# Attention units of eight heads in place of four, with the softmax denominators as products of their own

## The chip, the cores and the metric

One core of one Trainium2 chip. The metric is device time in microseconds (us) for one execution of the whole program; lower is better.

## The reference

```python
for c in range(S // 32):                      # chunked attention, B=2, H=8, S=768, D=64
    k_full = concat(mem_k, k[c*32-16 : c*32+40])   # 8 memory keys and up to 56 others
    a = exp(scale * q_c @ k_full.T - max)
    out[c] = (a / (a.sum() + 1e-9)) @ v_full
x = out as (1536 tokens, 512)
x = sum_e p[:, e] * (relu(x @ w1[e]) @ w2[e])      # 4 experts, F = 1024
h = x @ w_in                                       # 512 -> 2048
y = (max(h, 0) + alpha * min(h, 0)) @ w_out
```

All values are float32. The matrix products after attention are made from high and low parts in a reduced form of float32 (names ending in h and l), three products for each, and the first of each pair by a scheme of seven block products in place of eight, which needs sums of token blocks (`st`) and of weight blocks (`s`).

## The kernel before, in words

**Attention.** 1536 tokens are 12 units of 128 (`u`), each with 8 heads. A half unit (`half_unit`, line 221) takes four heads through these steps:

- S: 32 small matmuls on TensorE write the scores into the tile `two`, two banks of PSUM (the even heads in the first, the odd in the second), with 4 windows of 32 queries by 64 keys each. VectorE takes the maximum (`mx`) and writes the difference to `pe`.
- exp on ScalarE, in place.
- T: two transposes of `pe` into PSUM, copied to `pt` by ScalarE.
- X: 16 matmuls of `pt` with `v`. The tile of v holds a column of ones beside its 64 columns, so the denominators come out as column 64. VectorE adds 1e-9 (`dn`), inverts (`rd`) and scales to `xs`.
- XT: two transposes of `xs`, copied by ScalarE into `acc`, tokens as columns.

After the fourth half unit of a block of 256 tokens (two units, one block `c` of columns), `prep_x` (line 157) makes from `acc` the token operands `xh` and `xl` of the first expert product: ScalarE rounds, VectorE makes four sums in `st`, GpSimd (POOL) or VectorE the low parts. `pt`, `xs` and `pe` are rings of two (line 205), `qk` of four half units, `v` of three. The tile `two` is one buffer in both kernels.

**Order of the work.** Every engine executes in the order in which the program emits. `att_cycle` (line 332) emits the first part: scores of half unit m, XT of m-3, X of m-2, exp of m, then four or five filler products (`keep_warm`, line 150, whose results nobody reads), then T of m-1. It runs until the first three blocks of columns are done, which takes 16 cycles. After that the first expert tile (0, 384 columns) begins. Its 42 products of `gemm1` (line 601) and 48 of `gemm2` (line 688) each call `att_poll` (line 296) first, which emits whatever step of the remaining half units is due by a running sum of assumed costs (`now`, `T_S`, `LAT`, `PACE` and so on, lines 878 to 886). `clear` and `NEED` say which stage of one half unit has to follow which of an earlier one. The loop at line 842 drains what is left before the second tile begins.

**Queues.** All loads go out on SP's queue in program order: `load_half` (q and k of a half unit) after S, `load_v` after X, and the other tiles by the list `begun` (line 818), which counts half units begun. The first expert weights (`raw`) are prepared by POOL and ScalarE during attention (`prep_w1`, line 412).

Of the kernel before, what the change touches and what calls it, by code (L numbers as in the profile page):

```python
# [20 lines left out]
BLK = 128  # L21
# [14 lines left out]
QW, KW, VW = HP * BLK, HP * SPAN, HP * (D + 1)  # L36
# [29 lines left out]
def tile_kernel(ctx: ExitStack, tc: tile.TileContext, qk, v, wa, wq, dpt, alpha, out):  # L66
# [83 lines left out]
    def keep_warm(hu):  # L150

        o = bank(f"keep{hu}")[:, :NCOL // 2]
# [4 lines left out]
    def prep_x(c0, n, fast):  # L157
# [5 lines left out]
        e = dve if fast else pool  # L163
        sub = ALU.subtract
        act.copy(xh[:, 0:4, cs], acc[:, :, 0, cs])
        dve.tensor_tensor(out=st[:, 0], in0=b12, in1=b11, op=sub)
        yield
        dve.tensor_tensor(out=st[:, 1], in0=b22, in1=st[:, 0], op=sub)
        act.copy(xh[:, 4:6, cs], b22)
        yield  # L170
        dve.tensor_tensor(out=st[:, 2], in0=b22, in1=b12, op=sub)
        pool.tensor_tensor(out=xl[:, 0:4, cs], in0=acc[:, :, 0, cs], in1=xh[:, 0:4, cs].bitcast(F32), op=sub)
        yield
        for z in (0, 1):
            r = slice(6 + 4 * z, 10 + 4 * z)
# [8 lines left out]
            (e if fast or z else dve if c0 == 2 * BLK else pool).tensor_tensor(  # L184
                out=xl[:, r, cs], in0=t_, in1=xh[:, r, cs].bitcast(F32), op=sub)
            yield

    def transition(c0, n):
        yield now[0] + X_WAIT[c0 > 0], None
        for d0 in range(c0, c0 + n, BLK):  # L190
            for _ in prep_x(d0, BLK, True):
                yield now[0] + DT_X[c0 > 0], None

    def mm(*a, n, took=None, **kw):
# [5 lines left out]
    v_t = [bp.tile([P, 2, HP, NW, D + 1], F32, name=f"v{i}", **tag) for i, tag in enumerate(  # L200
        [dict(tag="w2", bufs=4)] * 2 + [dict(tag="fr")])]
# [3 lines left out]
    pt_ring, xs_ring, pe_ring = (bp.tile([P, 2, HP * BLK], F32, tag="ft", bufs=3, name=x) for x in ("pt", "xs", "pe"))  # L205
    pt_ring = pt_ring.rearrange("p r (z q) -> p r z q", q=BLK)
    xs_ring = xs_ring.rearrange("p r (z e d) -> p r z e d", e=2, d=D)
    pe_ring = pe_ring.rearrange("p r (z k e) -> p r z k e", e=2, k=KEYS)
# [5 lines left out]

    def load_v(hu):
        if hu >= 2 * NU:
            return
        for e in range(2):
            sync.dma_start(v_t[hu % RINGV][e::2, e].rearrange("p z w d -> p (z w d)"), v[hu // 2, e, :, hu % 2])

    def half_unit(u, half):

        hu = 2 * u + half
        qv = qk_t[hu % RING][:, :QW].rearrange("p (z q) -> p z q", q=BLK)
        kv = qk_t[hu % RING][:, QW:].rearrange("p (z k) -> p z k", k=SPAN)
        vv = v_t[hu % RINGV]
# [8 lines left out]
        for z in range(HP):
            for w in range(NW):
                for e in range(2):
                    rows = slice(e * D, (e + 1) * D)
                    mm(s_ps[win[w], e, z], qv[rows, z, win[w]], kv[rows, z, w * STEP:w * STEP + KEYS], n=KEYS,
                       took=T_S, start=True, stop=True)  # L240
        load_half(hu + RING)
        mx = cp.tile([P, 2, HP], F32, tag="mx", bufs=4, name=f"mx{nm}")
        dve.tensor_reduce(out=mx, in_=s_ps, axis=AX.X, op=ALU.max)
        pe = pe_ring[:, hu % 2]
        dve.tensor_tensor(
            out=pe.rearrange("p z k e -> p e z k"), in0=s_ps,
            in1=mx.unsqueeze(3).to_broadcast([P, 2, HP, KEYS]), op=ALU.subtract,
# [4 lines left out]
        t_ps = bank(f"t{nm}")[:, :HP * BLK].rearrange("p (z q) -> p z q", q=BLK)  # L252
        now[0] += T_SW
        for z in range(HP):
            pe_.transpose(t_ps[:, z], pe[:, z].rearrange("p k e -> p (k e)"), ident)
            now[0] += T_T
        pt = pt_ring[:, hu % 2]
        act.copy(pt, t_ps)
        yield LAT[1]
        x_ps = bank(f"x{nm}")[:, :2 * VW].rearrange("p (z e d) -> p z e d", e=2, d=D + 1)  # L260
        now[0] += T_SW
        for z in range(HP):
            for w in range(NW):
                mm(x_ps[win[w], z], pt[:, z, win[w]], vv[:, :, z, w], n=2 * (D + 1), took=T_X, start=True, stop=True)
        load_v(hu + RINGV)
        dn = cp.tile([P, HP, 2, 1], F32, tag="dn", bufs=2, name=f"dn{nm}")
        dve.tensor_scalar_add(dn, x_ps[:, :, :, D:D + 1], 1e-9)
        rd = cp.tile([P, HP, 2, 1], F32, tag="rd", bufs=2, name=f"rd{nm}")
        dve.reciprocal(rd, dn)
        xs = xs_ring[:, hu % 2]  # L270
        dve.tensor_tensor(out=xs, in0=x_ps[:, :, :, :D], in1=rd.to_broadcast([P, HP, 2, D]), op=ALU.mult)
        yield LAT[2]
        xt_ps = bank(f"xt{nm}")[:, :2 * BLK].rearrange("p (c q) -> p c q", q=BLK)
        now[0] += T_SW
        for z in range(HP):
            pe_.transpose(xt_ps[:, z], xs[:, z].rearrange("p e d -> p (e d)"), ident)
            now[0] += T_T
        act.copy(acc[:, hs, ab, cols], xt_ps)
        if ab == 1 and half == 1:
            while att["x"] < c:  # L280
                yield 0.2
            for _ in prep_x(c * BLK, BLK, c in FAST):
# [3 lines left out]
    att = {"next": 0, "start": 0.0, "done": 0, "over": set(), "live": [], "x": 0, "stage": [0] * (2 * NU + 1)}

    NEED = {0: 3, 2: 4}

    def clear(hu):  # L290
        if att["stage"][hu] == 3 and hu > 1 and att["stage"][hu - 2] < 5:
            return False
        return hu < 2 or att["stage"][hu - 2] >= NEED.get(att["stage"][hu], 0)


    def att_poll(force=False):

        while True:
            due = [x for x in att["live"] if x[0] <= now[0] and clear(x[2])]
            room = att["next"] < 2 * NU and len(att["live"]) < LIVE and clear(att["next"])  # L300
# [11 lines left out]
            elif room and att["start"] <= now[0]:  # L312
                g = half_unit(*divmod(att["next"], 2))
# [17 lines left out]

    def att_cycle():
# [14 lines left out]
        def at(hu, stage):  # L347
            if hu in live and att["stage"][hu] == stage:
                advance(live[hu])

        x = live[m] = [now[0], half_unit(*divmod(m, 2)), m]
# [100 lines left out]
    def prep_w2(p):  # L452
# [5 lines left out]
        if p == 1:  # L458
            yield pause(0.0, lambda: att["done"] == 2 * NU and (1, 1) in raws)
# [344 lines left out]
    for k in range(kc + 9, len(tiles)):  # L804
# [3 lines left out]
    load_half(0)  # L808
    load_half(1)
    load_v(0)  # L810
    load_half(2)
    load_half(3)
    load_v(1)
    load_v(2)
# [21 lines left out]
    for i, (what, k, *other) in enumerate(order):  # L836
# [3 lines left out]
        if what == 1:  # L840
            if p == 0:
                while att["done"] < 4 * -(-(c0 + n) // BLK):
# [4 lines left out]
                    prep_poll()  # L847
                    begin()
# [49 lines left out]
RINGV = 3  # L898
# [75 lines left out]
```

## Time and profile before

| | |
|---|---|
| median of 3 runs | 833.89 us (832.63 to 834.43) |
| the profiled execution's own time | 834.19 us |
| its span, first to last instruction | 832.4 us |
| granted clock of TensorE | 1.00 of full speed (2.4 GHz) |
| TensorE, VectorE, ScalarE, GpSimd busy | 98%, 71%, 40%, 68% |

The span is shorter than the time by what lies around the program. In the timelines of the profile a row gives the start, the time from there to the end of the last of its instructions, the engine, the operation with the tile that is written and those that are read, the count, and in brackets the engine's idle time before it and what ended it. TensorE's matmuls are pipelined and their ends are modelled, so the distance from one start to the next tells more than a duration. Nearly all instructions bear line 60, that of a helper which records every operation; the tiles' names tell them apart.

### The profile page before, as it was taken

To read this page: it belongs to the slowest core of one execution; us is meant where nothing else is said; L and a number is where in the kernel's file an instruction comes from. 1 tells how busy PE (TensorE), PEld (TensorE's weight loads), DVE (VectorE), ACT (ScalarE), POOL (GpSimd) and SP (SyncE) were. 2 spreads that over 40 slices of the span, in tenths; PEclk is the share of its full clock that TensorE was granted. 3 is DMA by queue.
4 is the path that set the end of the run, shared out by engine and by line. 5 is a ranking of instruction groups with operands and counts; after the bars stand their busy time and mean duration, and the time that the engine had idled before them with its cause. 6 is when DMAs were issued, how large, how long until landed. Compare 5 with 4: busy or idle time off the path is not lost.

```text
span 832.4 us, 15024 instructions
## 1 busy us (share of the span) xinstructions
PE 817.8 (98%) x5659; PEld 794.4 (95%) x5659; DVE 592.2 (71%) x1151; ACT 335.5 (40%) x754; POOL 563.0 (68%) x584
## 2 busy tenths in 40 slices
PE   9988999999999999999999999999999999999998
PEld 6656999999999999999999999999899999999998
DVE  5878656876786776876777767568964877756555
ACT  3655542322322332332232333144663756456432
POOL 2746767868878878878687773183955887866611
PEclk9999999999999999999999999999999999999999
DMA  8794102323223223223323302001002142211004
GB/s 243 214 275 121 52 26 92 102 99 101 89 65 101 89 80 124 89 64 102 102 90 102 113 27 73 30 23 54 27 4 98 52 118 74 76 53 51 1 0 152
DMA packets 30504, 71.70 MB, mean 86 GB/s; under 512 B 4704, under 2 KB 9952, under 8 KB 30432
## 3 DMA queue, kind: packets, MB, share of 16 engines
q1 hardware_dynamic: 30432, 70.75, 26.5%
q8 instruction: 44, 0.72, 0.4%
q14 instruction: 28, 0.23, 0.1%
HBM read 59.18 MB, written 11.56 MB: 85 GB/s over the span
## 4 chain that ended last, share of the span: by engine, by line
PE 86%; DVE 5%; POOL 4%; ACT 2%; issue 1%; DMA 1%; SPq 0%; DVEq 0%; POOLq 0%; ACTq 0%
PE y L60 46%; PE a L60 11%; PE c L60 11%; PE d L60 10%; PE b L60 5%; POOL xl L60 1%; DVE st L60 1%; POOL gg L60 1%; DMA raw<-in_wa 1%; POOL wl L60 1%; ACT g L60 1%; PE x L60 1%; POOL s L60 1%; PE keep L60 1%; DVE xs L60 1%
## 5 line engine op out<-in xcount | busy, mean ns | idle before, releaser
L60 PE MATMUL y<-gg,wh 128*128 128x384 f32 x1540 | 400.7, 337 | 0.6 <-POOL gg L60 0.4
L60 POOL TENSOR_TENSOR gg<-g,gg 128x384 fp32r<-128x384 f32 x192 | 202.0, 1062 | 125.0 <-ACT gg L60 112.7
L60 PEld LDWEIGHTS y<-gg,wh 128*128 128x128 f32 x1540 | 279.2, 188 | 1.8 <-POOL gg L60 1.6
L60 PE MATMUL y<-gg,wl 128*128 128x384 f32 (+1 forms) x770 | 259.2, 337 | 0.0
L60 DVE TENSOR_TENSOR acc<-y,acc 128x384 f32<-128x384 f32 x321 | 170.2, 549 | 51.0 <-PE y L60 49.4
L60 ACT CAST gg<-g 128x384 fp32r<-128x384 f32 x192 | 97.6, 511 | 171.6 <-DVE g L60 171.4
L60 POOL TENSOR_TENSOR wl<-raw,wh 128x256 fp32r<-128x256 f32 (+1 forms) x112 | 114.9, 1034 | 52.5 <-ACT wh L60 39.9
L60 PEld LDWEIGHTS y<-gg,wl 128*128 128x128 f32 x770 | 144.5, 188 | 0.0
L60 ACT COPY u<-a 128x384 f32<-128x384 f32 x48 | 23.0, 478 | 181.8 <-PE a L60 181.8
L60 POOL TENSOR_TENSOR wl<-s,wh 128x256 fp32r<-128x256 f32 x88 | 68.0, 779 | 6.9 <-ACT wh L60 6.7
L60 DVE TENSOR_TENSOR u<-b,u 128x384 f32<-128x384 f32 x48 | 26.7, 556 | 57.1 <-PE b L60 53.3
L60 PE MATMUL a<-xh,wh 128*128 128x384 f32 x184 | 62.3, 339 | 0.5 <-ACT u L60 0.5
L60 PE MATMUL d<-xh,wh 128*128 128x384 f32 x184 | 62.2, 338 | 0.0
L60 PE MATMUL a<-xl,wh 128*128 128x384 f32 x184 | 62.0, 337 | 0.0
L60 PE MATMUL a<-xh,wl 128*128 128x384 f32 x184 | 61.9, 336 | 0.0
L60 PE MATMUL d<-xh,wl 128*128 128x384 f32 x184 | 61.8, 336 | 0.0
L60 PE MATMUL d<-xl,wh 128*128 128x384 f32 x184 | 61.8, 336 | 0.0
L60 ACT CAST wh<-raw 128x256 fp32r<-128x256 f32 (+1 forms) x116 | 54.5, 491 | 14.8 <-PE y L60 14.2
L60 PE MATMUL c<-xh,wh 128*128 128x384 f32 x176 | 59.5, 338 | 0.3 <-DVE b L60 0.3
L60 PE MATMUL c<-xh,wl 128*128 128x384 f32 x176 | 59.4, 337 | 0.0
L60 POOL TENSOR_TENSOR fl<-fl,fm 128x512 f32<-128x512 f32 x32 | 41.4, 1293 | 26.4 <-DVE fm L60 17.5
L60 PE MATMUL c<-xl,wh 128*128 128x384 f32 x176 | 59.2, 336 | 0.0
(111 smaller groups left out, 1398.4 us busy)
## 6 DMA issues: line engine op xcount, KB each, us to landing
fr<-in_wq SPq DMA_DIRECT2D x32, 512.0 KB, 3.9
raw<-in_wa SPq DMA_DIRECT2D x28, 512.0 KB, 3.8
w2s<-fl SPq DMA_DIRECT2D x32, 256.0 KB, 2.4
raw<-w2s SPq DMA_DIRECT2D x16, 512.0 KB, 3.7
qk<-in_qk SPq DMA_DIRECT2D x24, 312.0 KB, 4.2
v<-in_v SPq DMA_DIRECT2D x48, 130.0 KB, 4.0
outT<-acc SPq DMA_DIRECT2D x15, 192.0 KB, 1.9
pb<-p_dram SPq DMA_DIRECT2D x6, 384.0 KB, 3.3
```

The source lines that it names most:

```text
L60: return self.tc.keep_in_program_order(f(*a, **kw))
```

## The change

- A unit of eight heads (`unit`) takes the place of two half units. Each stage has 64 matmuls, 4 transposes or 32 matmuls, and one operation of 512 columns on VectorE or ScalarE where there were two of 256. `pt`, `xs` and `pe` have one buffer each.
- v loses its column of ones. The denominators are made by matmuls of their own (D) from `pt` and a tile `sel` of two columns of ones over the even and the odd keys; units at the ends of a sequence use other columns in the first or last window, and 16 matmuls in place of four. They are written to columns 256 to 263 of the first bank of `two`, beside the scores.
- In a cycle: scores of m, D and X of m-1, exp of m, fillers (ten in the first cycle, four in the others), T of m, XT of m-1.
- The token sums `st` read XT's result in PSUM for the odd unit of a block; only two of its four rows of 128 are kept in `acc` as they are, and the last sums overwrite the other half of `acc`.
- v has four buffers for the first 16 half units and three after. The list `begun` counts units. Some constants of the emitter's costs change.

```diff
-    def keep_warm(hu):
+    def keep_warm(u):
...
-        for i in range(5 if hu < 3 else 4):
+        for i in range(4 if u else 10):
...
+    sel = []
+    for name, k0, k1 in (("inner", 0, KEYS), ("first", LEFT, KEYS), ("last", 0, KEYS - RIGHT)):
+        sel.append(cp.tile([P, 2], F32, name=name))
+        dve.tensor_reduce(out=sel[-1], in_=ident[:, 2 * k0:2 * k1].rearrange("p (k e) -> p e k", e=2),
+                                axis=AX.X, op=ALU.add)
+    pt, xs, pe = (bp.tile([P, 2 * HP * BLK], F32, tag="ft", bufs=3, name=x) for x in ("pt", "xs", "pe"))
...
+    def unit(u):
...
+        n_s = 2 * HP * KEYS
+        s_ps = two[:, :, :n_s].rearrange("p e (z k) -> p e z k", k=KEYS)
+        d_ps = two[:, 0, n_s:n_s + 4 * HP]
         now[0] += T_SW
+        for half in range(2):
...
+                        mm(s_ps[win[w], e, HP * half + z], qv[rows, z, win[w]], kv[rows, z, w * STEP:w * STEP + KEYS],
+                           n=KEYS, took=T_S, start=True, stop=True)
+            load_half(2 * u + half + RING)
+        mx = cp.tile([P, 2, 2 * HP], F32, tag="mx", bufs=2, name=f"mx{u}")
         dve.tensor_reduce(out=mx, in_=s_ps, axis=AX.X, op=ALU.max)
         dve.tensor_tensor(
             out=pe.rearrange("p z k e -> p e z k"), in0=s_ps,
+            in1=mx.unsqueeze(3).to_broadcast([P, 2, 2 * HP, KEYS]), op=ALU.subtract,
         )
         yield LATE
         act.activation(pe, pe, AF.Exp, scale=scale)
         yield LAT[0]
...
         act.copy(pt, t_ps)
         yield LAT[1]
         now[0] += T_SW
+        for z in range(2 * HP):
+            d = d_ps[:, 2 * z:2 * z + 2]
+            if 0 < j < NBLK - 1:
+                mm(d, pt[:, z], sel[0], n=2, took=T_D, start=True, stop=True)
+            else:
+                for w in range(NW):
+                    edge = 1 if j == w == 0 else 2 if j == NBLK - 1 and w == NW - 1 else 0
+                    mm(d[win[w]], pt[:, z, win[w]], sel[edge], n=2, took=T_D / NW, start=True, stop=True)
...
+                mm(x_ps[win[w], z], pt[:, z, win[w]], v_of(2 * u + half)[:, :, i, w], n=2 * D, took=T_X,
+                   start=True, stop=True)
+            if i == HP - 1:
+                while v_next[0] < V_FOUR and v_next[0] <= 2 * u + half + 4 or v_next[0] <= 2 * u + half + 3:
+                    load_v(v_next[0])
+        dve.tensor_scalar_add(dn, d_ps, 1e-9)
...
+        if ab == 0:
+            act.copy(first, xt_ps)
+            yield X_STEP[c]
             while att["x"] < c:
                 yield 0.2
+            act.copy(xh[:, 0:4, cols], first)
+            yield X_STEP[c]
+            pool.tensor_tensor(out=xl[:, 0:4, cols], in0=first, in1=xh[:, 0:4, cols].bitcast(F32), op=sub)
+            return
+        st = bp.tile([P, 3, 2, BLK], F32, tag="st", name=f"st{u}")
+        b12, b22 = xt_ps[:, 0:2], xt_ps[:, 2:4]
+        act.copy(st[:, 2], b22)
+        dve.tensor_tensor(out=st[:, 0], in0=b12, in1=acc[:, 0:2, 0, cols], op=sub)
+        if c not in FAST:
+            yield X_STEP[c]
+        dve.tensor_tensor(out=st[:, 1], in0=b22, in1=st[:, 0], op=sub)
+        act.copy(xh[:, 4:6, cols], st[:, 2])
+        dve.tensor_tensor(out=acc[:, 2:4, 1, cols], in0=st[:, 2], in1=b12, op=sub)
+        yield X_STEP[c]
...
+        (dve if c in FAST else pool).tensor_tensor(
+            out=xl[:, 10:14, cols], in0=acc[:, :, 1, cols], in1=xh[:, 10:14, cols].bitcast(F32), op=sub)
+        att["x"] = c + 1
+    NEED = {0: 3, 2: 4, 3: 5}
+    def clear(u):
+        return u == 0 or att["stage"][u - 1] >= NEED.get(att["stage"][u], 0)
...
+        x = live[m] = [now[0], unit(m), m]
...
         advance(x)
-        at(m - 3, 4)
-        at(m - 2, 3)
+        at(m - 1, 3)
         at(m, 1)
+        rest()
         keep_warm(m)
-        at(m - 1, 2)
+        at(m, 2)
+        at(m - 1, 4)
         now[0] = max(now[0], t0 + PACE0)
+        rest()
...
-LAT = (1.0, 0.8, 1.6)
-LATE = 1.3
-T_S, T_X, T_T, T_SW = 0.017, 0.06, 0.11, 0.1
-FAST = (5,)
+LAT = (1.1, 1.0, 1.9)
+LATE = 1.6
+T_S, T_X, T_T, T_SW, T_D = 0.018, 0.06, 0.11, 0.1, 0.1
+FAST = (2, 5)
-PACE = 1.9
-PACE0 = 2.2
-X_STEP = (1.2, 0.8, 0.4, 1.0, 1.0, 0.4)
-PREP0 = 13.5
+PACE = 3.8
+PACE0 = 3.9
+X_STEP = (0.8, 0.8, 0.0, 0.8, 0.8, 0.8)
+PREP0 = 11.0
-RINGV = 3
+V_FOUR = 16
```

## Rows read from the trace of the kernel before

**Rows 1.** The page: engines' busy time, granted clock by slice

```profile
PE 817.8 (98%) x5659; PEld 794.4 (95%) x5659; DVE 592.2 (71%) x1151; ACT 335.5 (40%) x754; POOL 563.0 (68%) x584
...
PEclk9999999999999999999999999999999999999999
```

**Rows 2.** Busy time by stretch: length, engines with instructions, clock, DMA share, GB/s

```profile
4.92:47.10 42.18, 38.95 (x860) 28.37 (x859) 32.00 (x86) 22.36 (x61) 21.07 (x26) 1.00 0.83 243
47.10:85.53 38.43, 33.12 (x547) 25.30 (x547) 30.85 (x74) 22.36 (x58) 22.41 (x20) 1.00 0.57 176
85.53:832.40 746.87, 741.80 (x4237) 738.19 (x4236) 527.78 (x988) 289.32 (x634) 516.14 (x528) 1.00 0.22 72
...
8.00:16.00 8.00, 7.85 (x173) 5.94 (x171) 5.11 (x17) 3.42 (x9) 0.00 (x0) 1.00 0.95 283
72.00:80.00 8.00, 5.29 (x41) 3.93 (x40) 7.70 (x15) 3.40 (x9) 5.29 (x6) 1.00 0.20 59
```

**Rows 3.** Timeline of TensorE (PE), one cycle of stage A and the scores before

```profile
11.25 0.45 PE L60 MATMUL two<-qk 64*32 64x64 f32 x32
...
13.41 0.38 PE L60 MATMUL t<-ident,pe 128*128 128x128 f32 x2
13.72 0.45 PE L60 MATMUL two<-qk 64*32 64x64 f32 x32
14.11 0.44 PE L60 MATMUL xt<-ident,xs 128*128 128x128 f32 x2
14.47 0.65 PE L60 MATMUL x<-v,pt 128*32 128x130 f32 x16
15.05 0.97 PE L60 MATMUL keep<-xh 128*128 128x384 f32 x4
15.86 0.38 PE L60 MATMUL t<-ident,pe 128*128 128x128 f32 x2
```

**Rows 4.** Timeline of TensorE: the longest wait of stage A

```profile
22.92 0.65 PE L60 MATMUL x<-v,pt 128*32 128x130 f32 x16 [1.01 <-DMA v<-in_v]
```

**Rows 5.** Waits, 0 to 90 us: us in total, times, longest

```profile
PE xt L60 <- DVE xs L60: 4.5, 7, 1.9
...
PE two L60 <- issue: 1.9, 2, 1.4
```

**Rows 6.** Chain that ended last: start, duration, two transposes and six products

```profile
13.57 0.22 PE t L60 x2
...
85.70 1.05 PE a L60 x6
```

**Rows 7.** Groups of instructions by form, 0 to 110 us: busy, mean ns, idle

```profile
L60 PE MATMUL keep<-xh 128*128 128x384 f32 x67 | 16.6, 372 | 0.0
...
L60 DVE TENSOR_TENSOR xs<-x,rd 128x256 f32<-128x256 f32 x24 | 10.2, 424 | 0.8
L60 ACT ACTIVATE pe<-pe 128x256 f32<-128x256 f32 x24 | 10.1, 419 | 12.9 <-DVE pe L60 11.2 <-DVE dn L60 1.7
...
L60 ACT CAST xh<-acc 128x512 fp32r<-128x512 f32 x6 | 3.8, 628 | 0.0
...
L60 DVE TENSOR_TENSOR t<-d,u 128x384 f32<-128x384 f32 x3 | 1.7, 554 | 0.4 <-PE d L60 0.3
```

**Rows 8.** Timelines of VectorE, and of TensorE behind one difference

```profile
11.84 0.42 DVE L60 TENSOR_REDUCE mx<-two 128x4 f32<-128x256 f32 x1 [0.80 <-PE two L60]
12.37 0.42 DVE L60 TENSOR_TENSOR pe<-two,mx 128x256 f32<-128x256 f32 x1
...
29.08 0.35 DVE L60 TENSOR_REDUCE mx<-two 128x4 f32<-128x256 f32 x1
29.46 0.42 DVE L60 TENSOR_TENSOR pe<-two,mx 128x256 f32<-128x256 f32 x1
...
29.94 0.46 PE L60 MATMUL two<-qk 64*32 64x64 f32 x32 [0.33 <-DVE pe L60]
...
43.21 1.45 DVE L60 TENSOR_TENSOR st<-acc,st 128x256 f32<-128x256 f32 x1
```

More of the change, by code (lines that the diff above doesn't have):

```diff
@@ L148, in tile_kernel, with prep_x @@
     nc.gpsimd.memset(xh[:, 10:14, spare].bitcast(F32), 0.0)
-    def keep_warm(hu):
-        o = bank(f"keep{hu}")[:, :NCOL // 2]
+    def keep_warm(u):
+        o = bank(f"keep{u}")[:, :NCOL // 2]
         now[0] += 0.1
-        for i in range(5 if hu < 3 else 4):
+        for i in range(4 if u else 10):
             mm(o, xh[:, 10 + i % 4, NCOL // 2:NCOL // 2 + P], xh[:, 13, spare], n=NCOL // 2, start=True, stop=True)
-    def prep_x(c0, n, fast):
+    def prep_x(c0, n):
         cs = slice(c0, c0 + n)
@@ L190, in transition @@
         for d0 in range(c0, c0 + n, BLK):
-            for _ in prep_x(d0, BLK, True):
+            for _ in prep_x(d0, BLK):
                 yield now[0] + DT_X[c0 > 0], None
@@ L199, in tile_kernel @@
     qk_t = [bp.tile([P, QW + KW], F32, tag="ggB", bufs=4, name=f"qk{i}") for i in range(RING)]
-    v_t = [bp.tile([P, 2, HP, NW, D + 1], F32, name=f"v{i}", **tag) for i, tag in enumerate(
-        [dict(tag="w2", bufs=4)] * 2 + [dict(tag="fr")])]
+    v_t = [bp.tile([P, 2, HP, NW, D], F32, name=f"v{i}", **tag) for i, tag in (
+        (3, dict(tag="w2", bufs=4)), (0, dict(tag="w2", bufs=4)), (1, dict(tag="w2", bufs=4)), (2, dict(tag="fr")))]
+    v_t = v_t[1:] + v_t[:1]
     for vt in v_t:
@@ L204, in tile_kernel, with v_of @@
             (pool, dve)[e].memset(vt[:, e], 0.0)
[L205 to L208, printed above, removed]
+    sel = []
[4 more added lines that the diff above has]
+    pt, xs, pe = (bp.tile([P, 2 * HP * BLK], F32, tag="ft", bufs=3, name=x) for x in ("pt", "xs", "pe"))
+    pt = pt.rearrange("p (z q) -> p z q", q=BLK)
+    xs = xs.rearrange("p (z e d) -> p z e d", e=2, d=D)
+    pe = pe.rearrange("p (z k e) -> p z k e", e=2, k=KEYS)
+    def v_of(hu):
+        return v_t[hu % 4 if hu < V_FOUR else (hu - V_FOUR) % 3]
     def load_half(hu):
@@ L218, in load_v @@
         for e in range(2):
[L219 to L226, printed above, removed]
+            sync.dma_start(v_of(hu)[e::2, e].rearrange("p z w d -> p (z w d)"), v[hu // 2, e, :, hu % 2])
+    def unit(u):
@@ L227, in half_unit @@
         c, ab = divmod(u, 2)
+        j = u % NBLK
         cols = slice(c * BLK, (c + 1) * BLK)
-        hs = slice(2 * half, 2 * half + 2)
-        nm = f"{u}_{half}"
         win = [slice(w * WIN, (w + 1) * WIN) for w in range(NW)]
-        s_ps = two[:, :, :HP * KEYS].rearrange("p e (z k) -> p e z k", k=KEYS)
+        n_s = 2 * HP * KEYS
+        s_ps = two[:, :, :n_s].rearrange("p e (z k) -> p e z k", k=KEYS)
+        d_ps = two[:, 0, n_s:n_s + 4 * HP]
         now[0] += T_SW
[L235 to L240, printed above, removed]
@@ L241, in half_unit @@
-        load_half(hu + RING)
-        mx = cp.tile([P, 2, HP], F32, tag="mx", bufs=4, name=f"mx{nm}")
+        for half in range(2):
+            qk_ = qk_t[(2 * u + half) % RING]
+            qv = qk_[:, :QW].rearrange("p (z q) -> p z q", q=BLK)
+            kv = qk_[:, QW:].rearrange("p (z k) -> p z k", k=SPAN)
+            for z in range(HP):
+                for w in range(NW):
+                    for e in range(2):
+                        rows = slice(e * D, (e + 1) * D)
+                        mm(s_ps[win[w], e, HP * half + z], qv[rows, z, win[w]], kv[rows, z, w * STEP:w * STEP + KEYS],
+                           n=KEYS, took=T_S, start=True, stop=True)
+            load_half(2 * u + half + RING)
@@ L251, in half_unit @@
         yield LAT[0]
-        t_ps = bank(f"t{nm}")[:, :HP * BLK].rearrange("p (z q) -> p z q", q=BLK)
+        t_ps = bank(f"t{u}").rearrange("p (z q) -> p z q", q=BLK)
         now[0] += T_SW
-        for z in range(HP):
+        for z in range(2 * HP):
             pe_.transpose(t_ps[:, z], pe[:, z].rearrange("p k e -> p (k e)"), ident)
             now[0] += T_T
-        pt = pt_ring[:, hu % 2]
         act.copy(pt, t_ps)
         yield LAT[1]
-        x_ps = bank(f"x{nm}")[:, :2 * VW].rearrange("p (z e d) -> p z e d", e=2, d=D + 1)
@@ L261, in half_unit @@
         now[0] += T_SW
-        for z in range(HP):
-            for w in range(NW):
[L264 to L270, printed above, removed]
@@ L271, in half_unit @@
-        dve.tensor_tensor(out=xs, in0=x_ps[:, :, :, :D], in1=rd.to_broadcast([P, HP, 2, D]), op=ALU.mult)
+        for z in range(2 * HP):
+            d = d_ps[:, 2 * z:2 * z + 2]
+            if 0 < j < NBLK - 1:
+                mm(d, pt[:, z], sel[0], n=2, took=T_D, start=True, stop=True)
+            else:
+                for w in range(NW):
+                    edge = 1 if j == w == 0 else 2 if j == NBLK - 1 and w == NW - 1 else 0
+                    mm(d[win[w]], pt[:, z, win[w]], sel[edge], n=2, took=T_D / NW, start=True, stop=True)
@@ new lines, in unit @@
+        x_ps = bank(f"x{u}").rearrange("p (z e d) -> p z e d", e=2, d=D)
+        for z in range(2 * HP):
+            half, i = divmod(z, HP)
+            for w in range(NW):
+                mm(x_ps[win[w], z], pt[:, z, win[w]], v_of(2 * u + half)[:, :, i, w], n=2 * D, took=T_X,
[3 more added lines that the diff above has]
+                    load_v(v_next[0])
@@ L272, in half_unit @@
+        dn = cp.tile([P, 4 * HP], F32, tag="dn", bufs=2, name=f"dn{u}")
+        dve.tensor_scalar_add(dn, d_ps, 1e-9)
+        rd = cp.tile([P, 2 * HP, 2, 1], F32, tag="rd", bufs=2, name=f"rd{u}")
+        dve.reciprocal(rd.rearrange("p z e o -> p (z e o)"), dn)
+        dve.tensor_tensor(out=xs, in0=x_ps, in1=rd.to_broadcast([P, 2 * HP, 2, D]), op=ALU.mult)
         yield LAT[2]
-        xt_ps = bank(f"xt{nm}")[:, :2 * BLK].rearrange("p (c q) -> p c q", q=BLK)
+        xt_ps = bank(f"xt{u}").rearrange("p (c q) -> p c q", q=BLK)
@@ L274, in half_unit @@
         now[0] += T_SW
-        for z in range(HP):
+        for z in range(2 * HP):
             pe_.transpose(xt_ps[:, z], xs[:, z].rearrange("p e d -> p (e d)"), ident)
             now[0] += T_T
-        act.copy(acc[:, hs, ab, cols], xt_ps)
-        if ab == 1 and half == 1:
+        sub = ALU.subtract
+        first = acc[:, :, 0, cols]
+        if ab == 0:
+            act.copy(first, xt_ps)
+            yield X_STEP[c]
             while att["x"] < c:
                 yield 0.2
-            for _ in prep_x(c * BLK, BLK, c in FAST):
-                yield X_STEP[c]
-            att["x"] = c + 1
@@ L286, in tile_kernel @@
[L286 to L293, printed above, removed]
+            act.copy(xh[:, 0:4, cols], first)
+            yield X_STEP[c]
+            pool.tensor_tensor(out=xl[:, 0:4, cols], in0=first, in1=xh[:, 0:4, cols].bitcast(F32), op=sub)
@@ new lines, in unit @@
+        yield X_STEP[c]
+        while att["x"] < c:
+            yield 0.2
+        act.copy(xh[:, 6:10, cols], st[:, 0:2].rearrange("p a b n -> p (a b) n"))
+        dve.tensor_tensor(out=acc[:, 0:2, 1, cols], in0=acc[:, 2:4, 0, cols], in1=st[:, 1], op=sub)
+        pool.tensor_tensor(out=xl[:, 4:6, cols], in0=st[:, 2], in1=xh[:, 4:6, cols].bitcast(F32), op=sub)
+        yield X_STEP[c]
+        pool.tensor_tensor(out=xl[:, 6:10, cols], in0=st[:, 0:2].rearrange("p a b n -> p (a b) n"),
+                           in1=xh[:, 6:10, cols].bitcast(F32), op=sub)
@@ new lines, in unit @@
+        act.copy(xh[:, 10:14, cols], acc[:, :, 1, cols])
+        yield X_STEP[c]
+        (dve if c in FAST else pool).tensor_tensor(
+            out=xl[:, 10:14, cols], in0=acc[:, :, 1, cols], in1=xh[:, 10:14, cols].bitcast(F32), op=sub)
+        att["x"] = c + 1
+    att = {"next": 0, "start": 0.0, "done": 0, "over": set(), "live": [], "x": 0, "stage": [0] * (NU + 1)}
+    NEED = {0: 3, 2: 4, 3: 5}
+    def clear(u):
+        return u == 0 or att["stage"][u - 1] >= NEED.get(att["stage"][u], 0)
@@ L299, in att_poll @@
             due = [x for x in att["live"] if x[0] <= now[0] and clear(x[2])]
-            room = att["next"] < 2 * NU and len(att["live"]) < LIVE and clear(att["next"])
+            room = att["next"] < NU and len(att["live"]) < LIVE and clear(att["next"])
             if due:
@@ L312, in att_poll @@
             elif room and att["start"] <= now[0]:
-                g = half_unit(*divmod(att["next"], 2))
+                g = unit(att["next"])
                 att["start"] = now[0] + (PACE0 if force else PACE)
@@ L339, in advance @@
             try:
-                x[0] = next(x[1]) + (now[0] if att["stage"][x[2]] < 6 else x[0])
+                x[0] = next(x[1]) + now[0]
             except StopIteration:
@@ L345, in advance, with at, rest @@
                     att["done"] += 1
[L347 to L351, printed above, removed]
+        def at(u, stage):
+            if u in live and att["stage"][u] == stage:
+                advance(live[u])
+        def rest():
+            for x in list(att["live"]):
+                if att["stage"][x[2]] > 4 and x[0] <= now[0]:
+                    advance(x)
+            prep_poll()
+            begin()
+        x = live[m] = [now[0], unit(m), m]
         att["live"].append(x)
@@ L458, in prep_w2 @@
         if p == 1:
-            yield pause(0.0, lambda: att["done"] == 2 * NU and (1, 1) in raws)
+            yield pause(0.0, lambda: att["done"] == NU and (1, 1) in raws)
         if p:
@@ L806, in tile_kernel @@
     order += [(2, len(tiles) - 1)]
[L808 to L814, printed above, removed]
+    for hu in range(RING):
+        load_half(hu)
+    for hu in range(4):
+        load_v(hu)
     stream("w", weights())
@@ L841, in tile_kernel @@
             if p == 0:
-                while att["done"] < 4 * -(-(c0 + n) // BLK):
+                while att["done"] < 2 * -(-(c0 + n) // BLK):
                     if k == 0:
@@ L846, in tile_kernel @@
                         att_poll(force=True)
-                    prep_poll()
-                    begin()
+                        prep_poll()
+                        begin()
             if k == k0 - 1:
@@ L940 @@
     qk = np.concatenate([halves(qs, BLK), halves(ks, SPAN)], axis=3)
[L941 removed]
+    vs = vs.reshape(NU, KEYS, 2, HP, 2, NW, D).transpose(0, 4, 1, 2, 3, 5, 6)
     def pairs(wi, wo):
```

45 lines of the change are left out of this document (19 added, 26 removed).

## The prediction, on record before the kernel ran

> **What bounds the kernel now.** I read the page first: TensorE is busy 98% of the span, and its granted clock is at full speed (2.4 GHz) in every slice [rows 1]. Next the three stretches into which the change divides the span [rows 2]. From 85.53 us on TensorE's gaps are short: 741.80 us busy in 746.87. That stretch holds none of the changed code, so I carry it over unchanged; what the change earns or costs must appear before 85.53 us. Stage A, 4.92 to 47.10, is attention with filler products; stage B, 47.10 to 85.53, is the rest of attention threaded through the 90 products of the first expert tile. No other engine is full in either stage (VectorE 32.00 us of 42.18 and 30.85 of 38.43).
>
> Then TensorE's timeline. A cycle of stage A is one half unit and has five groups, read from start to start [rows 3]: transposes of pe 0.31 us (13.41 to 13.72), scores S 0.39, transposes of xs 0.36, products X 0.58, four fillers 0.81: together 2.45. Two halves, one unit of eight heads, cost 4.90. Sixteen cycles run from 4.92 to 47.10; the stage's few waits are of 1 us and less, the longest for v [rows 4]. In B the gaps are larger: four of the seven waits for xs, 3.7 of their 4.5 us, and one of 1.4 that has no releaser [rows 5]; the dense work there is 8 S, 9 T, 10 X, 11 XT and 90 products at 1.05/6 = 0.175 each [rows 6]: 3.1 + 2.8 + 5.8 + 4.0 + 15.8 = 31.5. Of the 38.43 us, 5.1 are the gaps named, and 1.8 is left for changes between short groups.
>
> **Part 1: whole units.** S has 64 matmuls (2 x 0.39 = 0.77 rounded down), X 32 (1.16). Each further transpose costs 0.11 (two in 0.22 [rows 6]), so T is 0.31 + 0.22 = 0.53 and XT 0.58. Fillers stay four, 0.81, but per unit: 38 in stage A against 67 [rows 7].
>
> On VectorE a 256-wide operation takes 0.42 and a 384-wide one 0.55 [rows 7], 1.0 ns an element, so a 512-wide one 0.68. Exp on ScalarE goes from 0.42 to about 0.63, the figure of a 512-wide rounding there, and the copies with it [rows 7]. Per unit VectorE saves about 0.8 us on maxima, differences, reciprocals and scaling, and some on token sums, which it now reads half from PSUM. That relief I count at nothing on the path: VectorE needs 0.68 x 3 + 0.16 + 0.18 = 2.4 us a unit and at most three sums of 0.8, 4.8 in all, against the cycle of 5.88 below. It is covered by the wait of part 2; without that cover it would show as in rival 1.
>
> **Part 2: the denominators' products D.** This is where I expect the loss. D(m-1) writes columns 256 to 263 of the first bank of tile `two`. In program order it follows S(m), and the maximum and difference of unit m, which read that bank. If the tile is guarded as a bank, D(m-1) waits until VectorE has finished the difference of unit m. TensorE takes its instructions in order, so X(m-1), the fillers, T(m) and XT(m-1) queue behind D, and ScalarE (pt, the token copies), VectorE's xs and the v loads on SP's queue behind those.
>
> The length of that wait comes from one half unit [rows 8, 3]. S starts at 11.25, the maximum at 11.84: 0.59 later, and with 32 more matmuls 0.97. The difference starts 0.53 after the maximum; 512-wide 0.79, so at 1.76. It ends 0.68 later, at 2.44. The tightest handover from this difference to TensorE is 29.88 to 29.94, so D can begin at 2.50. S has issued by 0.77: TensorE stands 1.73 us in every unit.
>
> D itself isn't in the trace: four matmuls with 128x128 weights and 2 columns (16 with 128x32 weights in the edge units 0, 5, 6 and 11). Lower bound 0.05 (the pitch of S, 0.39/32, four times), upper bound 0.58 (16 at the pitch of X). I take 0.30, near the middle: the nearest row, a transpose at 0.11, loads the same weights but moves 128 columns. The ones column leaves X, whose pitch I keep (128 columns for 130).
>
> Cycle: 0.77 + 1.73 + 0.30 + 1.16 + 0.81 + 0.53 + 0.58 = 5.88, against 4.90. Exp has ended at 2.44 + 0.68 = 3.1, so T, reached at 4.8, waits for nothing; xs is ready 0.7 after X, within the fillers and T.
>
> **Sum of A.** Eight cycles again: unit 5 must be over before the first expert product, with its last token part on VectorE, after unit 7's T. The first cycle has no D: S, then ten fillers while exp is made, T at 3.15, end at 3.68. Seven at 5.88 make 41.2. One us I add for the three or four token sums of unit 5 that come together ahead of unit 7's maximum (one took 1.45 here [rows 8]). Together 45.9 against 42.18: **+3.7**.
>
> **Sum of B.** Left are 4 S, 4 T, 5 D, 5 X, 5 XT and the products: 3.1 + 2.1 + 1.5 + 5.8 + 2.9 + 15.8 = 31.2; changes between groups 1.0 (fewer groups). Working the emitter's costs through by hand, D(8) follows directly on S(9) (1.73), D(9) and D(10) have an XT between (1.15 each), the other two have no S before them: 4.0. VectorE also carries the expert tile there (7.70 us of 8 in its fullest stretch [rows 2]), and may be inside one operation when a maximum comes due: 0.4 on each of the three, 1.2. Of the old gaps I keep half of the 1.4 and a quarter of the waits for xs: 1.7. Together 39.1 against 38.43: **+0.6**.
>
> **Edits costed at nothing.** DMA: a unit brings 2 x 312 KB of qk and 4 x 128 KB of v, 1.16 MB; over 5.88 us that is 198 GB/s, and 283 were moved in one stretch [rows 2]. Raw weights are asked for somewhat earlier, behind four instead of three pairs of v loads, and the POOL queue that waits for them is idle then; expert weights for the next tile are asked for one half unit later, and TensorE's 90 products cover that. One more v buffer adds two memsets, and three short sums make `sel`; both run before the first scores arrive. POOL takes one 1.3 us subtraction more in the last block, off the path.
>
> 834.19 (the profiled run's own time; its span is 832.4) + 3.7 + 0.6 = 838.5. That run was 0.3 above the median of 833.89, so **838.2**.
>
> **Rival 1, faster: D doesn't wait.** D's columns are not the ones VectorE reads, and if the guard goes by columns nothing holds it. For this speaks that the fillers read `xh` with 0.0 idle while ScalarE writes other columns of the same tile [rows 7]; against it, that this tile is in SBUF, and that the trace has no product entering a part of a PSUM tile while another part is read. Then TensorE's cycle is 4.15, or 4.26 with T held until exp (3.15 + 0.06). A: 3.68 + 7 x 4.26 + 1.0 = 34.5, -7.7. B loses the 4.0: 35.1, -3.3. 834.19 - 11.0 - 0.3 = 822.9. Traffic (1.16 MB in 4.26 us = 272 GB/s) would then be the next limit. The deciding place is the start of D against the end of the difference. Chance 0.15.
>
> The Trainium skill, "PSUM — Partial Sum Buffer", section "PSUM bank collisions raise a hardware error", speaks against this change: two engines on one bank and quadrant have to be separated by a semaphore even at different columns. By that rule D waits and the sum is 838.2; without it 822.9. No row here shows it.
>
> **Rival 2, a wash: the wait is there but all my short groups are dear.** If D costs 0.05, VectorE's second operation follows 0.1 sooner (as at 29.46, 0.38 after 29.08 [rows 8]) and B's backlog and old gaps don't come back, then 12 x 0.25 + 12 x 0.1 + 1.7 = 5.9 us fall away: 832.3. The middle of that stretch, about 834, is where the removed fillers (29 x 0.2 = 5.8 us) just pay for D and the wait. For it: VectorE sets several gaps of the kernel before. Against: these were only 3.7 us in B. Chance 0.22, of it 0.13 within 0.2%, which is what a measurement can tell from no change (1.7 us), and 0.09 below.
>
> **Rival 3, much slower: the clock falls.** TensorE would stand 29% of each cycle. In 72 to 80 us it was busy 5.29 of 8 at full clock [rows 2], so I give 0.03; at 1.2 GHz some 4 us of work a unit would double, up to +30 us, about 868.
>
> **How the numbers follow.** Forecast (bank guarded, over 0.2% slower) 0.60, rival 1 0.15, rival 2 0.22, rival 3 0.03. Slower 0.63, same 0.13, faster 0.24. The forecast alone spans 835.6 to 844 (D at 0.58 in twelve units, +3, and another 2 to 3 of backlog). The range goes down to 826, so that it holds rival 2 and leaves rival 1 and the far end out.
>
> **What would show it.** Right: in the waits, D on TensorE ended by VectorE's difference, 1.7 us each, some ten times; a unit's cycle near 5.9; fillers 38; first expert product near 51 us; the pass to the second tile near 90. Wrong: D starting before the difference ends and a cycle near 4.3 (rival 1); v or qk waits on TensorE (the traffic); a cycle below 5.4 (rival 2).

## The result and the profile after the change

The changed kernel took 846.46 us (median of 4 runs, 843.22 to 849.30) against 834.16 for the kernel before: ratio 1.0142, interval [1.0094, 1.0190]. Run again among the experiments it gave 846.14, ratio 1.0140 [1.0109, 1.0171]. It is 12 us slower; 838.2 was forecast, with 844 as the end of the range. The profiled execution took 847.47 us, 13.3 more than the profiled one of before. (The profiled execution of one experiment, e10, was a disturbed one of 1627.67 us; only the times of its other three are used.)

The page of the changed kernel, the lines that answer to [rows 1]:

```profile
PE 820.8 (97%) x5822; PEld 805.9 (95%) x5822; DVE 575.7 (68%) x1094; ACT 331.2 (39%) x718; POOL 562.2 (66%) x586
...
PEclk8689999999999999999999999999999999999999
```

The clock is the first thing that is different: the first three slices are below 0.9 of full speed. Next the busy time in three stretches, as in [rows 2]: stage A to the end of its eighth cycle (64.12), the rest of attention with the first expert tile (to 104.51), and everything after; then eight microseconds of stage A in two halves.

```profile
4.92:64.12 59.20, 46.17 (x963) 39.67 (x962) 23.47 (x51) 19.88 (x41) 20.99 (x27) 0.77 0.65 194
64.12:104.51 40.39, 34.21 (x606) 30.46 (x607) 25.32 (x49) 21.15 (x44) 22.00 (x20) 1.00 0.42 129
...
104.51:845.70 741.19, 736.43 (x4237) 733.16 (x4236) 524.39 (x985) 288.67 (x632) 515.40 (x528) 1.00 0.22 73
...
16.00:20.00 4.00, 2.33 (x77) 2.18 (x78) 1.38 (x2) 1.89 (x4) 0.41 (x1) 0.85 0.76 206
20.00:24.00 4.00, 4.00 (x41) 3.40 (x41) 1.06 (x3) 0.00 (x0) 3.84 (x7) 0.50 0.41 128
```

Stage A took 59.2 us (42.2 before, 45.9 forecast) at a mean clock of 0.77; four microseconds of it ran wholly at 0.50, which is 1.2 GHz. Stage B took 40.4 (38.4 before, 39.1 forecast). The last stretch, where I expected no difference, became 5.7 us shorter with the same 4237 matmuls. 17.0 + 2.0 - 5.7 = 13.3.

TensorE's timeline shows the mechanism: first a cycle whose X and fillers run at 1.2 GHz, then parts of one at full speed.

```profile
25.11 1.06 PE L60 MATMUL two<-qk 64*32 64x64 f32 x64
27.77 1.02 PE L60 MATMUL two<-inner,pt 128*128 128x2 f32 x8 [1.60 <-DVE pe L60]
28.73 1.69 PE L60 MATMUL x<-v,pt 128*32 128x128 f32 x32
30.34 1.65 PE L60 MATMUL keep<-xh 128*128 128x384 f32 x4
...
50.22 0.86 PE L60 MATMUL two<-qk 64*32 64x64 f32 x64
52.75 0.20 PE L60 MATMUL two<-inner,pt 128*32 128x2 f32 x3 [1.67 <-DVE pe L60]
...
55.79 0.91 PE L60 MATMUL two<-qk 64*32 64x64 f32 x64
```

D stands behind VectorE's difference of the next unit, 1.60 and 1.67 us, where 1.73 was forecast. The cycle from 50.22 to 55.79, at full clock, took 5.57. In the other cycles the fillers take 1.65 and not 0.97 us, and a cycle lasts up to 9.2 (33.09 to 42.30). VectorE on one such wait:

```profile
26.21 0.69 DVE L60 TENSOR_REDUCE mx<-two 128x8 f32<-128x512 f32 x1 [0.16 <-PE two L60]
26.93 0.69 DVE L60 TENSOR_TENSOR pe<-two,mx 128x512 f32<-128x512 f32 x1
28.83 0.17 DVE L60 TENSOR_SCALAR dn<-two 128x8 f32<-128x8 f32 x1 [1.21 <-PE two L60]
```

The difference ends at 27.62 (26.93 + 0.69), D starts at 27.77, as if guarded by the bank; e2 below tests that. The Trainium skill, "PSUM — Partial Sum Buffer", section "PSUM bank collisions raise a hardware error", asks for a guard by bank and quadrant, and the 1.60 us agree with a program that keeps to it; no run here shows the collision itself. In total, from the table of waits, 0 to 110 us:

```profile
PE two L60 <- DVE pe L60: 16.3, 10, 2.7
PE y L60 <- POOL gg L60: 1.4, 1, 1.4
...
PE y L60 <- ACT gg L60: 0.8, 1, 0.8
```

Ten waits: seven in stage A (the longest, 2.7, where unit 5's token sums come first) and three in stage B, 1.39, 1.20 and 1.09. My sum had ten too. The two waits for `gg`, which the second expert product reads, lie in stage B and were in no sum of mine.

### The profile page after: what moved, and what is told of

Read it like the earlier page. It is cut to its first block, busy times and chain, and to the rows that moved or that the text cites. A ratio compares the mean times of both kernels' runs of the same rounds, so it can differ in the third digit from the quotient of the medians.

```text
span 845.7 us, 15236 instructions
## 1 busy us (share of the span) xinstructions
PE 820.8 (97%) x5822; PEld 805.9 (95%) x5822; DVE 575.7 (68%) x1094; ACT 331.2 (39%) x718; POOL 562.2 (66%) x586
## 4 chain that ended last, share of the span: by engine, by line
PE 93%; DVE 3%; POOL 2%; ACT 2%; issue 1%; DVEq 0%; ACTq 0%
PE y L60 46%; PE a L60 12%; PE c L60 11%; PE d L60 11%; PE b L60 6%; PE two L60 2%; PE x L60 2%; PE keep L60 1%; DVE pe L60 1%; DVE mx L60 1%; POOL gg L60 1%; PE t L60 1%; ACT g L60 1%; POOL xl L60 1%; PE wps0.0_84 L60 0%
```

## The experiments

Times are medians, ratios are to the kernel before on the same chip (e5, e6, e7 and e9 ran on one chip, e12 on a second, the others on a third). Start points are read from TensorE's timelines: of the first expert product (49.41 us before, 67.14 after) and of the second tile's first product (85.53 and 104.51).

**e1: fillers in the wait.** The clock tested by itself: the wait stays, TensorE works in it. Filler results are used by nobody.

```diff
         yield LAT[1]
+        if u < 7:
+            h = bank(f"hole{u}")[:, :NCOL // 2]
+            for i in range(HOLE):
+                pe_.matmul(h, xh[:, 10 + i % 4, NCOL // 2:NCOL // 2 + P], xh[:, 13, spare], start=True, stop=True)
         now[0] += T_SW
         for z in range(2 * HP):
             d = d_ps[:, 2 * z:2 * z + 2]
...
+HOLE = 8
```

> Eight more fillers (1.6 us) stand on TensorE just before each D of stage A, in the 1.67 us in which it waited for VectorE. Theory A (the wait of D costs its own 1.7 us a unit, and besides lets the granted clock fall to 1.2 GHz, which makes the work after it twice as long): the cycles keep the wait's length but the clock stays at 1.00, a cycle takes 5.6 us with the windowed D and 6.3 with the whole one, stage A 46 to 47 us in place of 59.2, the kernel about 834. Theory B (the clock falls for another reason, such as the small matmuls or the start-up): the clock is below 0.9 again from 12 to 64 us and the time stays at 843 or more.

839.83 us, ratio 1.0053 [1.0032, 1.0074]. TensorE's timeline, one cycle:

```profile
21.38 0.86 PE L60 MATMUL two<-qk 64*32 64x64 f32 x64
22.17 1.66 PE L60 MATMUL hole<-xh 128*128 128x384 f32 x8
23.96 1.02 PE L60 MATMUL two<-inner,pt 128*128 128x2 f32 x8
24.92 1.08 PE L60 MATMUL x<-v,pt 128*32 128x128 f32 x32
25.93 0.97 PE L60 MATMUL keep<-xh 128*128 128x384 f32 x4
...
27.70 0.91 PE L60 MATMUL two<-qk 64*32 64x64 f32 x64
```

The clock is 1.00 in all of 4.92 to 56.83, a cycle takes 6.3, and the first expert product starts at 56.83 in place of 67.14. More work on TensorE made the kernel 6.6 us faster: theory A holds, B falls. Stage A is 48.0 us (its eighth cycle ends at 52.87), a little over the 46 to 47 expected, with 1.19 of a wait left in the last cycle. The time is 840 and not 834 also because stage B, where no fillers were added, is 2.4 us longer than in the changed kernel: TensorE stood 0.79 us with no releaser that the profile shows, and behind a wait of 1.39 the clock fell once, to 0.79 on average from 64 to 72 us.

**e3: D by windows.**

```diff
-            if 0 < j < NBLK - 1:
+            if False:
                 mm(d, pt[:, z], sel[0], n=2, took=T_D, start=True, stop=True)
             else:
```

> D is made by windows (16 matmuls with 128x32 weights) in every unit, not in the edge units alone; it stays in the scores' bank and keeps its wait. In the profile of the changed kernel the windowed D took 0.25 us, the whole one 0.95. If D's own length lies on the path: 8 units x 0.7 = 5.6 us less, somewhat more where the clock is low, so 838 to 841. If it is covered by something: 845 to 847 as before this edit.

840.63, ratio 1.0077 [1.0051, 1.0102]: 5.8 us less than the changed kernel, as if D lay wholly on the path. The trace shows the whole D as eight instructions with 128x128 weights (two for each of the code's four matmuls) that take 0.96 us (27.77 to 28.73 above), and the windowed one as 32 with 128x32 in 0.25 to 0.36 at full clock.

**e9: both.** e1's fillers and e3's windows leave of the change what the prediction had assumed: the wait, a full clock and a short D.

> Fillers in the wait of D, as in e1, and D by windows, as in e3: the two prices that the prediction had wrong, the clock and D's length, are both set to what it assumed (full clock, D about 0.3 us), and the wait for the bank is left. If the rest of its sum holds, stage A is 45 to 47 us and the time 834 to 839 (e1's 839.8 less 8 x 0.7 = 834.2). If another term is wrong too, stage A is off by more than 2 us and the time above 840 or below 832.

834.53, ratio 1.0002 [0.9987, 1.0016]. The second tile starts at 90.25, 4.7 us later than before; the forecast for A and B together was +4.3. Its stretches and the wait that ends stage A (at 51.40 - 0.24 = 51.16: 46.2 us for A, 45.9 forecast; 39.1 for B, 39.1 forecast):

```profile
4.92:53.47 48.55, 45.50 (x1244) 38.63 (x1243) 24.45 (x54) 20.98 (x43) 22.57 (x28) 1.00 0.80 240
...
90.25:832.10 741.85, 736.81 (x4237) 733.10 (x4236) 524.39 (x985) 288.54 (x632) 515.34 (x528) 1.00 0.23 73
...
51.40 0.43 PE L60 MATMUL two<-inner,pt 128*32 128x2 f32 x32 [0.24 <-ACT pt L60]
```

That its time equals the kernel's before is the last stretch again: 741.85 against 746.87.

**e2: a bank of its own for D.**

```diff
-    ps = ctx.enter_context(tc.tile_pool(name="ps", bufs=6, space=bass.MemoryType.PSUM))
+    ps = ctx.enter_context(tc.tile_pool(name="ps", bufs=5, space=bass.MemoryType.PSUM))
...
+    den = sc.tile([P, 512], F32, tag="den", name="den")
...
-        if more and taken[0] % 4 == 0:
+        if more and taken[0] % 8 in (0, 3, 6):
...
-        more.append(ctx.enter_context(tc.tile_pool(name="pm", bufs=2, space=bass.MemoryType.PSUM)))
+        more.append(ctx.enter_context(tc.tile_pool(name="pm", bufs=3, space=bass.MemoryType.PSUM)))
...
-        d_ps = two[:, 0, n_s:n_s + 4 * HP]
+        d_ps = den[:, :4 * HP]
```

> D writes a PSUM bank of its own; five banks in place of six rotate during attention. Theory A (the wait is for the bank, not for the data): no wait of D for VectorE's difference, clock 1.00, a cycle of 4.3 to 4.8 us, stage A 37 us in place of 59.2, stage B 4 us shorter, the kernel 819 to 823. Theory C (one buffer a stage or the v and qk traffic would hold the whole units anyway): other waits of 1 us and more a cycle take the place of D's, and the time is 830 or more.

824.66, ratio 0.9875 [0.9848, 0.9901]: faster than both kernels, and the fastest of this study. The order of the instructions is unchanged; the waits for the difference are gone:

```profile
14.25 0.86 PE L60 MATMUL two<-qk 64*32 64x64 f32 x64
15.04 1.05 PE L60 MATMUL den<-inner,pt 128*128 128x2 f32 x8
16.02 1.08 PE L60 MATMUL x<-v,pt 128*32 128x128 f32 x32
...
18.82 0.86 PE L60 MATMUL two<-qk 64*32 64x64 f32 x64
```

A cycle is 4.57 (two of the old ones are 4.90), and the first expert product starts at 47.05. So disjoint columns did not free D; another bank did. Theory C is not what holds it, though other waits come up (1.5 us for exp in the last cycle, 1.7 for v). The time is above theory A's 819 to 823: in the profiled execution, at 828.25 the slowest of its four, the clock fell three times, behind waits of 1.51, 1.65 and 1.44 us.

**e6 and e8: D behind X, in the scores' bank.** X then fills 1.0 us of the wait. e8 also makes D by windows.

```diff
-        for z in range(2 * HP):
-            d = d_ps[:, 2 * z:2 * z + 2]
...
         x_ps = bank(f"x{u}").rearrange("p (z e d) -> p z e d", e=2, d=D)
...
+        for z in range(2 * HP):
+            d = d_ps[:, 2 * z:2 * z + 2]
...
         dn = cp.tile([P, 4 * HP], F32, tag="dn", bufs=2, name=f"dn{u}")
```

> D stays in the scores' bank, but is emitted behind X: the 1.0 us of X stands in the wait. By theory A what is left of the wait is 1.7 - 1.0 = 0.7 us a unit, the clock stays at 1.00 behind so short a hole, a cycle takes 4.9 to 5.2 us with the whole D, stage A 40 us and the kernel 825 to 830. If the clock falls behind 0.7 us too: 834 and more. xs now waits for D, not for X; if that shows, XT waits for xs, some 0.3 us a unit.

> D behind X as in e6 (829.9) and by windows as in e3, in the scores' bank. If D's length is on the path, 8 x 0.7 = 5.6 us less than e6: 824. If the traffic bounds stage A by now (e5 and e7 stand at 827), 826 to 829.

e6: 829.90, ratio 0.9938 [0.9914, 0.9962]. The waits are 0.50 to 0.61 us, with one of 1.65 in the last cycle, and the clock stays at 1.00 through stage A. Moving eight lines earns 16 us. e8: 829.61, 0.9954 [0.9936, 0.9971]: the short D brings nothing here. In its profile TensorE stood 0.96, 0.80 and 0.85 us in stage A with no releaser, and the clock fell once, to 0.62 from 20 to 24 us.

**e5 and e7: own bank and windows; and two fillers in place of four.**

> D in a bank of its own, as in e2, and by windows in every unit: no wait and the short D. If D's length lies on the path here too, 8 x 0.7 = 5.6 us below e2's 824.7: 819. If the chain from scores to exp (3.2 us, against S + D + X + fillers of 0.8 + 0.3 + 1.0 + 0.8 = 2.9) or the v and qk traffic takes its place, less than 3 us: 822 to 825.

> As e5, with two fillers a unit in place of four. If TensorE bounds stage A, 7 x 0.4 = 2.8 us less than e5. If the chain to exp bounds it (T waits for exp), no change; if the traffic does (1.16 MB a unit at about 285 GB/s = 4.1 us), waits for v or qk appear and nothing or less than 1 us is gained; and the clock may fall behind such waits, which would make it slower than e5.

e5 (own bank, windows): 827.66, 0.9916 [0.9901, 0.9931], no better than e2; e7 (the same with two fillers): 826.93, 0.9910 [0.9892, 0.9928]. Without the wait D's 5.6 us are no longer there to be had. e5's waits of TensorE, 0 to 90 us:

```profile
PE x L60 <- DMA v<-in_v: 4.1, 1, 4.1
PE t L60 <- ACT pe L60: 1.8, 2, 1.4
PE x L60 <- issue: 1.7, 2, 1.1
...
PE two L60 <- DMA qk<-in_qk: 0.9, 1, 0.9
```

The first product starts 1.2 us earlier than e2's, and one wait of 4.1 for v takes that and more away. In e7 (first product at 45.59) TensorE stands 6.9 us before X, D and S with no releaser that the profile shows, against 1.1 in e2: the fillers taken out turned into waits. Rival 1 named the traffic of v and qk as the next limit; e5's wait for v agrees, and what the unnamed waits are was not tried.

**e4: the kernel before without 52 of its 67 fillers.**

```diff
+        if hu >= 3:
+            return now.__setitem__(0, now[0] + 0.1 + 4 * 0.173)
         o = bank(f"keep{hu}")[:, :NCOL // 2]
...
-        for i in range(5 if hu < 3 else 4):
+        for i in range(5 if hu < 3 else 0):
```

> The kernel before without its fillers from the fourth half unit on (52 of 67 filler products left out; their results are used by nobody). If the clock falls only behind a hole of over a microsecond on TensorE, it stays at 1.00 here, and up to 52 x 0.2 = 10 us of fillers turn into waits for exp and VectorE: 826 to 834. If the clock follows the share of work, it falls in stage A (work 1.6 us in a cycle of 2 to 2.4) and the time is 838 or more.

835.58, ratio 1.0011 [0.9999, 1.0024]: neither of the two. Ten microseconds of fillers gone earned nothing. Some turned into waits (four of more than a microsecond in stage A), and the clock fell behind the longest, and again behind waits of 1.86 and 1.93 at 48.63 and 77.12. TensorE's timeline at that place, and two stretches:

```profile
27.64 0.44 PE L60 MATMUL t<-ident,pe 128*128 128x128 f32 x2
30.57 0.52 PE L60 MATMUL two<-qk 64*32 64x64 f32 x32 [2.49 <-DVE pe L60]
...
16.00:24.00 8.00, 4.95 (x142) 2.96 (x149) 5.26 (x16) 3.47 (x10) 3.40 (x6) 1.00 0.86 279
28.00:36.00 8.00, 5.20 (x104) 2.90 (x104) 5.54 (x16) 4.21 (x12) 4.20 (x6) 0.68 0.72 219
```

From 16 to 24 us TensorE was busy 4.95 of 8, with one wait of 1.99 for v, and the clock stayed; behind the wait of 2.49 it fell.

**e10 and e12: the v tiles at their old length.** Every kernel without the ones column has a last stretch of 741.2 to 742.1 us, the two with it 746.9 and 746.7. The v tiles share their slots with expert tiles, and 65 columns made those slots longer. e10 is the changed kernel, e12 is e2, each with the old length and 64 columns used.

```diff
-    v_t = [bp.tile([P, 2, HP, NW, D], F32, name=f"v{i}", **tag) for i, tag in (
+    v_t = [bp.tile([P, 2 * HP * NW * (D + 1)], F32, name=f"v{i}", **tag)[:, :2 * HP * NW * D].rearrange(
+        "p (e z w d) -> p e z w d", e=2, z=HP, w=NW) for i, tag in (
```

> The changed kernel with each v tile as long as in the kernel before (1040 values a partition, of which 1024 are used), so that the expert tiles which share these slots lie at the addresses of the kernel before. From the second tile's first product to the end the profiles took 746.9 and 746.7 us in the two kernels with the ones column and 741.2 to 742.1 in all seven without it, with the same products, at 0.175 against 0.174 us each. If the slots' length and so the place of the operands is the reason: that stretch is 746.5 to 747 again and the kernel 5 us slower than the changed one, about 851. If it is something else in the change: 741 to 742 and 846.

> D in a bank of its own (e2, 824.7) together with v tiles as long as in the kernel before (e10). If the slots' length sets the products' pitch, the stretch from the second tile's first product to the end is 746.5 to 747 us here, against e2's 741.6, and the time about 830; what is left against the kernel before, some 4 us, is then the gain of the units of eight heads alone. If e10 was slower for another reason: 741 to 742 and 825.

e10: 852.46 (the median of three times), ratio 1.0212 [1.0184, 1.0239], 6.3 above the changed kernel beside it. e12: 830.95, ratio 0.9976 [0.9954, 0.9997], and its last stretch:

```profile
83.14:830.40 747.26, 742.42 (x4237) 739.07 (x4236) 528.17 (x985) 288.85 (x632) 516.31 (x528) 1.00 0.23 72
```

747.26 against e2's 741.55. The slots' length makes the difference; whether by the place of the operands, and of which, was not tried. Of e2's gain over the kernel before, half and more is this (5.3 of 9.7 us); with the old length the units of eight heads, D in a bank of its own, earn 0.24% [0.03, 0.46].

**The changed kernel again.**

> The changed kernel itself, unaltered, beside the others on this chip, for its interval: 843 to 849, with the first expert product at 64 to 68 us and the stretch from the second tile on at 741 to 742.

846.14, first product at 63.56, second tile at 100.78, last stretch 741.82. In this execution the clock held behind two of the seven waits of stage A, in the first profile behind one; the second tile starts 3.7 us earlier.

## Why the prediction was right and where it failed

The direction and the wait were right: D waits for the maximum and the difference of the next unit (1.60 to 1.67 us, forecast 1.73), X, fillers, T and XT queue behind it, and stage B has three such waits. With the two prices set as the text assumed them (e9) stages A and B come out 0.3 and 0.0 us from its sums. For B that is partly luck: in e9 the three waits were 3.6 us (5.2 forecast, with VectorE's delays) and no wait for xs was left (1.7 kept with the old gaps), while the waits for `gg`, 2.2 us there too, were not in the sum.

The second tile's start adds up, one profile each: 85.53 before, +4.7 for the wait and the units of eight heads (e9, 90.25), +5.4 for D's length (e1, 95.64), +8.9 for the clock (104.51); then -5.7 in the last stretch. The split between D's length and the clock is rough, since e1's stage B has a fall of the clock in it and e11's second tile starts at 100.78, 5.1 behind e1's. By the medians, D's length is 5.3 us (e1 less e9; they ran on different chips, and by the ratios it is 4.3) and the clock 6.3 to 6.6 (the changed kernel's two medians less e1).

**The failed step is the clock.** Rival 3 had the mechanism, and a chance of 0.03 by the sentence "In 72 to 80 us it was busy 5.29 of 8 at full clock". That row shows one gap of 1.92 us among longer stretches of expert products, and the share of busy time that I compared does not tell: e4 stayed at full clock with 4.95 of 8. In the changed kernel the clock fell behind six of the seven waits of stage A, behind the first one already, and was back at 1.00 before the next wait began. The first two waits and what followed each:

```profile
8.80:11.34 2.54, 0.86 (x66) 0.73 (x66) 1.38 (x2) 0.70 (x2) 0.00 (x0) 1.00 0.88 252
11.34:15.95 4.61, 4.61 (x76) 3.97 (x76) 1.06 (x3) 0.78 (x2) 0.00 (x0) 0.63 0.95 325
15.95:18.48 2.53, 0.86 (x65) 0.72 (x65) 1.38 (x2) 0.92 (x3) 0.00 (x0) 1.00 0.70 160
18.48:25.11 6.63, 6.62 (x53) 5.69 (x53) 1.06 (x3) 1.61 (x3) 4.89 (x9) 0.52 0.55 167
```

The length of the gap alone does not tell either. The same wait of 1.44 us, at the end of stage B, left the clock alone in the changed kernel (first two rows) and lowered it in e2:

```profile
97.97 0.61 PE L60 MATMUL y<-gg,wh 128*128 128x384 f32 x2 [1.44 <-POOL gg L60]
96.00:104.00 8.00, 6.56 (x40) 6.31 (x39) 4.93 (x8) 6.15 (x15) 7.74 (x8) 1.00 0.00 1
...
76.86 0.61 PE L60 MATMUL y<-gg,wh 128*128 128x384 f32 x2 [1.44 <-POOL gg L60]
72.00:80.00 8.00, 5.98 (x27) 5.08 (x26) 6.81 (x11) 5.44 (x13) 8.00 (x8) 0.85 0.17 68
80.00:88.00 8.00, 8.00 (x45) 8.00 (x44) 2.34 (x2) 4.28 (x10) 3.51 (x5) 0.94 0.01 2
```

That the waits let the clock fall is shown by e1, which filled them; what decides behind which of them it falls stays open. I priced rival 3 as all or nothing (868); it came in part and cost 6 to 7 us by the medians.

**D was priced at 0.30 and took 0.96.** The upper bound of 0.58 was no bound. I named the row that had the answer, transposes at 0.11 with the same 128x128 weights, and took less since they move more columns. And I counted D by the matmuls of the code, while S and X are counted by the trace's instructions: [rows 3] show S as x32 where the code has 16 matmuls. D's four are eight in the trace; eight at 0.12 are 0.96. With it in the eight units that have the whole D the forecast would have been 5.3 us higher: 843.5.

**"I carry it over unchanged" was wrong by -5.7 us.** No instruction of the last stretch changed, but the length of the slots that its tiles share with v did (e10, e12). That the total missed by no more than 8.3 us is luck: this hid part of what D and the clock cost.

Rival 1's time, 822.9, was for a D that doesn't wait; e2 makes it so and took 824.7. It isn't a clean hit: D is longer than assumed, and the last stretch gives 5 us back. Rival 2's time, about 834, is e9's, but by luck: A and B took 4.7 us more (4.3 forecast), and the last stretch gave 5.0 back.

Relief on VectorE was counted at nothing. Its busy time in stage A fell from 32.00 to 23.47 us while the stage grew, and e9 came out at the sum without it; the old token sums were not put back alone, so its worth is not shown.

## What to carry to other kernels

Before putting a small result into the free columns of a PSUM bank, look at who reads that bank when the write comes due: here the guard covered the bank, and everything behind the write on TensorE waited too. A gap of 1.7 us in each cycle can cost more than its length, as the clock may fall behind it; test that by filling the gap with work nobody needs. Count instructions in the trace, not matmuls in the code, and check the stretches that hold none of the changed code: here a resized tile changed the pace of one that shares its slots.

## What was not expected of the hardware

- A float32 matmul with 128x128 weights and two columns takes 0.24 us (two instructions of 0.12 in the trace), the four of a unit 0.96; the same sums by 16 matmuls with 128x32 weights take 0.25 to 0.36.
- The clock held behind single gaps of 1.92 (before), 1.99 (e4), 2.78 (e3, at 54.08) and 1.44 us (changed kernel), and behind 0.5 to 0.6 in every cycle (e6). It fell behind single gaps of 1.39 (e1), 1.44, 1.51 and 1.65 (e2), 1.43 (e6) and 1.86, 1.93 and 2.49 (e4), and behind six of seven gaps of 1.60 to 2.73 in stage A of the changed kernel. The two sets overlap, so the length of a gap alone does not tell.
- The same 4237 expert matmuls take 741 to 742 or 747 us according to the length of slots that they share with tiles of an earlier stage, 0.7% of the stretch.
